# Crossbar DMA transposes in place of TensorE transposes, in a fused sparse-attention and squared-ReLU layer

## The chip, the cores and the metric

The kernel runs on one core of a Trainium2 chip. A core has five instruction streams: TensorE (PE, matrix products into PSUM), VectorE (DVE), ScalarE (ACT), GpSimd (POOL) and SyncE (SP), and sixteen DMA engines [...]. The metric is the device time of one execution in microseconds (us); lower is better.

## The reference

Two steps. First, attention over 4 batches, 8 heads, 768 positions and head size 64: a query attends to the 8 first (global) keys and to the 96 keys up to its own position, with a bias that falls linearly with distance. Then a two-layer network on the 3072 x 512 result.

```python
def _attn_ref(q, k, v, n_global, n_local):
    scores = scale * np.matmul(q, k.transpose(0, 1, 3, 2))
    rel = pos[:, None] - pos[None, :]
    is_global = pos[None, :] < int(n_global)          # 8
    is_local = (rel >= 0) & (rel < int(n_local))      # 96
    keep = is_global | is_local
    scores = scores + bias                            # -slope[h] * distance
    scores = np.where(keep, scores, -1000000000.0)
    a = softmax(scores)
    return np.matmul(a, v)

def _moe_ref(x, w_in, w_out):                         # 512 -> 2048 -> 512
    h = np.maximum(x @ w_in, 0.0)
    return h * h @ w_out
```

## The kernel before

The work is cut into eight half batches of 384 positions (three tiles of 128); the code calls one of them `x`, and `x.hb` is its number, 0 to 7. This text calls them h0 to h7. Heads are taken in four pairs (`a` from 0 to 3), since two heads of 64 fill 128 partitions.

For each half batch these steps follow:

- **Loads** (`list_loads`, line 279). Three tiles each of q, k and v are fetched from DRAM by DMAs issued on POOL, which turn fp32 into fp16. q and k go to staging tiles `sq` and `sk` (two buffers), v goes straight to its place. Each tile has position on the partitions.
- **Turning q and k** (`turn`, line 362). Scores need head size on the partitions. TensorE turns six 128 x 128 blocks per pair into a PSUM tile `trp`, and ACT or DVE copies it to `qk` (line 189 is the ACT copy, line 191 the copy on DVE or POOL). Then `fix_k` makes `kb`, on DVE: for each key tile a version in which the first 32 columns are those of tile 0, so that the global keys ride along with the local ones. `fix_v` does the same for v into `vb`, on POOL for h2 and later.
- **Scores and weights** (`score`, line 409). TensorE multiplies k and q blocks into `sp`, ACT takes the exponential (`ex`, line 424), and DVE multiplies by a precomputed mask (`phat`, lines 436 and 440).
- **Attending** (`attend`, line 464). TensorE multiplies by v, which carries a column of ones for the sum; DVE divides (`rec` and `tm`, lines 471 and 473).
- **Turning the output** (`to_x`, line 488). TensorE turns the three blocks of `tm` into a PSUM tile `trx`; ACT or DVE copies it to `xt`, which has features on the partitions.
- **Layer 1** (`layer1`, line 508): sixteen pieces of four matmuls each into `hps`, each piece needing all four pairs of `xt`; ReLU on ACT or DVE (lines 532 and 534), square on DVE (line 543).
- **Layer 2** (`layer2`, line 556): twelve pieces of four matmuls into `yps`; a copy to `y` and a store from SP (line 571).

h0 is worked tile by tile by functions of its own, and the order of everything for h0 and h1 up to 51.8 us is written out by hand (`OPENING`). After that a loop over half batches puts the layers of h*n* (`main`) beside the attention of h*n+1* (`side`); `merge` deals the attention's steps out between the pieces of the layers, and the loads for h*n+1* are listed ahead of it.

What order each engine gets is set by `Plan`. Every step is an `Op` with a price in us for each engine that may do it, a list of steps it needs, and a rank. TensorE's steps keep the order in which they were listed, and so do the loads; for the rest `run` repeatedly takes the step that can start first by those prices, with the lower rank first on a tie, and emits it on the cheapest engine. The prices are numbers in the code. On the chip every engine then runs its instructions in the emitted order, and waits for what each needs. `Ring` objects stand for PSUM buffers: six banks of `big`, two of `att`.

The loads of h*n* wait for the turning of h*n-2*, whose staging tiles they overwrite. In the line `before = [prev.turned[-1]] if prev else []` that is the last TensorE step of `turn`. A new batch's `qk`, `kb`, `v` and `vb` (two buffers) wait for the batch before last.

Of the kernel before, what the change touches and what calls it, by code (L numbers as in the profile page):

```python
# [8 lines left out]
FP32 = mybir.dt.float32  # L9
FP16 = mybir.dt.float16  # L10
# [3 lines left out]
P = 128  # L14
# [125 lines left out]
def kernel(  # L140
# [46 lines left out]
    def copy(e, out, in_):  # L187
        if e == "ACT":
            nc.scalar.copy(out=out, in_=in_)  # L189
        else:  # L190
            eng(e).tensor_copy(out=out, in_=in_)  # L191
# [75 lines left out]
    def list_loads(x):  # L267
        r0 = x.half * HALF
        prev = halves[x.hb - 2] if x.hb >= 2 else None
        before = [prev.turned[-1]] if prev else []  # L270
        vbefore = [halves[x.hb - x.half - 3].attended[-1]] if x.hb >= 4 else []

        def rows(src, name, t):
            def emit(e):
                if getattr(x, name, None) is None and name != "v":
                    setattr(x, name, stage_p.tile([P, HT, H, D], FP16, name=name, tag=name))
                dst = (x.bt.v[:, x.half * HT + t, :, 0:D] if name == "v"
                       else getattr(x, name)[:, t, :, :])
                nc.gpsimd.dma_start(out=dst, in_=src[x.b, :, r0 + t * P:r0 + (t + 1) * P, :]  # L279
                                    .rearrange("h p d -> p h d"))  # L280
            return plan.load(0.62, emit, vbefore if name == "v" else before)

        if x.half == 0:
            def start(e):
                new_batch(x.bt)
                nc.vector.memset(x.bt.v[:, :, :, D:D + 1], 1.0)
            x.bt.op = plan.add({"DVE": 0.1}, start, vbefore, rank=0)
        if x.hb:
            x.q_in = [rows(q, "sq", t) for t in range(HT)]
            x.k_in = [rows(k, "sk", t) for t in range(HT)]  # L290
            x.v_in = [rows(v, "v", t) for t in range(HT)]
        else:
            raw = {n: stage_p.tile([P, HT, H, D], FP32, name=n, tag=n, bufs=1)
                   for n in ("rq", "rk")}
            x.q_in, x.k_in, x.v_in = [], [], []

            def fetch(name, src, t, eng, e, lag):
                op = plan.add({e: 0.5}, lambda e: eng.dma_start(
                    out=raw[name][:, t], in_=src[0, :, t * P:(t + 1) * P, :].rearrange(
                        "h p d -> p h d")), rank=-1)  # L300
                op.lag = lag
                return op

            def cast(dst, name, t, f):
                def emit(e):
                    if getattr(x, dst, None) is None:
                        setattr(x, dst, stage_p.tile([P, HT, H, D], FP16, name=dst, tag=dst))
                    copy(e, getattr(x, dst)[:, t], raw[name][:, t])
                return plan.add({"DVE": 0.42, "ACT": 0.54}, emit, [f], rank=0)
            k0 = fetch("rk", k, 0, nc.scalar, "ACT", 3.5)  # L310
            q0 = fetch("rq", q, 0, nc.sync, "SP", 3.5)
            x.q_in.append(cast("sq", "rq", 0, q0))
            x.k_in.append(cast("sk", "rk", 0, k0))
            for t in range(HT):
                if t:
                    x.q_in.append(rows(q, "sq", t))
                    x.k_in.append(cast("sk", "rk", t, fetch("rk", k, t, nc.sync, "SP", 4.0 + t)))
                if t < 2:
                    x.v_in.append(rows(v, "v", t))
            x.v_in.append(rows(v, "v", 2))  # L320
        for l in x.v_in:
            l.needs.append(x.bt.op)
# [15 lines left out]
    def tiles_before(x):  # L338
        return (1, HT - 1) if x.half == 0 else (HT - 1, NT - 1)

    def fix_v(x):
# [9 lines left out]
        costs = {"POOL": 0.6 + 2.1 * n} if x.hb > 1 else {"DVE": 0.2 + 0.65 * n}  # L351
        x.vb_op = plan.add(costs, emit, x.v_in)

    def turn(x, a):
        state = {}

        def emit(e):
            state["ps"] = trp = ps_att.tile([P, 2, HT, P], FP16, name="trp", tag="att")
            warm(trp.rearrange("p i t c -> p (i t c)"))
            for i, st in enumerate((x.sq, x.sk)):  # L360
                for t in range(HT):
                    nc.tensor.transpose(out=trp[:, i, t, :], in_=st[:, t, 2 * a:2 * a + 2, :],  # L362
                                        identity=ident)
        job = plan.pe(6 * 0.056, emit, x.q_in + x.k_in + [ident_op], [att])

        def evac(i):
            def emit(e):
                copy(e, x.bt.qk[:, i, a, x.half * HALF:(x.half + 1) * HALF],
                     state["ps"][:, i].rearrange("p t c -> p (t c)"))
            return plan.after(job, {"ACT": 0.39, "DVE": 0.31}, emit)  # L370
        ops = [evac(0), evac(1)]
        t0, t1 = tiles_before(x)

        def fix_k(e):
            kt = x.bt.qk[:, 1, a, :].rearrange("p (t c) -> p t c", c=P)
            copy(e, x.bt.kb[:, a, t0 - 1:t1 - 1, GR:P], kt[:, t0:t1, GR:P])
            copy(e, x.bt.kb[:, a, t0 - 1:t1 - 1, 0:GR],
                 kt[:, 0:1, 0:GR].to_broadcast([P, t1 - t0, GR]))
        n = t1 - t0
        costs = {"DVE": 0.2 + 0.08 * n}  # L380
        if x.hb == 0:
            costs["POOL"] = 0.5 + 0.17 * n
        x.turned.append(job)
        x.qk_ops[a] = ops + [plan.add(costs, fix_k, [ops[1]])]

    GROUPS = {
        0: ([(0, 0), (1, 0), (1, 1)], [(2, 0), (2, 1)]),
# [91 lines left out]
    def to_x(x, a):  # L479
        st, norm = x.tm[a]  # L480

        def emit(e):
# [8 lines left out]
        x.x_ops[a] = plan.after(job, {"ACT": 0.39, "DVE": 0.31}, lambda e: copy(  # L491
            e, x.xt[:, a, :], st["trx"].rearrange("p t c -> p (t c)")))


    def layer1(x, ms, c0=0, c1=HALF, k0=0, k1=NCT):
        n = c1 - c0
# [52 lines left out]
    def layer2(x, j, m0):  # L549
        st = x.l2.setdefault(j, {})  # L550

        def emit(e):
            if m0 == 0:
                st["ps"] = ps_big.tile([P, 512], FP32, name="yps", tag="big")
            for m in range(m0, m0 + 4):
                nc.tensor.matmul(st["ps"], lhsT=x.h2[:, m, j * P:(j + 1) * P],  # L556
                                 rhs=w_out_sb[:, m, :], start=m == 0, stop=m == NFT - 1)
        job = plan.pe(4 * 0.216, emit, 
                      [x.h2_ops[max(c for c in x.h2_ops if c <= j * P)][m]
                       for m in range(m0, m0 + 4)] + [w_out_op[m0 // 4]], [big] if m0 == 0 else [])  # L560
        if m0 == 0:
            st["users"] = job.users
        else:
            job.users = st["users"]
            job.users[0].append(job)
        if m0 + 4 == NFT:
            def evac(e):
                y = y_p.tile([P, d_model], FP32, name="y", tag="y")
                copy(e, y, st["ps"])
                r0 = x.hb * HALF + j * P  # L570
                nc.sync.dma_start(out=out[r0:r0 + P, :], in_=y)
            plan.after(job, {"ACT": 0.52, "DVE": 0.63}, evac)

    for x in halves:
        x.turned, x.attended = [], []
# [97 lines left out]
    def tile_to_x(x, t, a0):  # L673
# [13 lines left out]
        for a in (a0, a0 + 1):  # L687
            x.x_ops[a, t] = op

    def attention(x):  # L690
        jobs = [lambda: fix_v(x)]
        for a in range(NPAIR + 3):
            if a < NPAIR:
                jobs.append(lambda a=a: turn(x, a))
            if 0 <= a - 1 < NPAIR:
                jobs.append(lambda a=a - 1: score(x, a))
            if 0 <= a - 2 < NPAIR:
                jobs.append(lambda a=a - 2: attend(x, a))
            if 0 <= a - 3 < NPAIR:
                jobs.append(lambda a=a - 3: to_x(x, a))  # L700
        return jobs

    def merge(main, side, start, stop):
        done = 0
        for i, f in enumerate(main):
            if i >= start:
                want = len(side) if i >= stop else (i - start) * len(side) // (stop - start)
                while done < want:
                    side[done]()
                    done += 1  # L710
            f()
        for f in side[done:]:
            f()

    def l1(x, m0=0):
        return [lambda m=m: layer1(x, [m]) for m in range(m0, NFT)]

    def l2(x):
        return [lambda j=j, m0=m0: layer2(x, j, m0) for j in range(HT) for m0 in range(0, NFT, 4)]
# [38 lines left out]
    for hb in range(1, NHB):  # L758
        x = halves[hb]
        if hb + 1 < NHB:  # L760
            list_loads(halves[hb + 1])
        main = l2(x0)[6:] + l2(x) if hb == 1 else l1(x) + l2(x)
        side = attention(halves[hb + 1]) if hb + 1 < NHB else []
        merge(main, side, 1, len(main) - 3)
    with tc.manual_schedule():
        order = plan.run()

# [34 lines left out]
```

The softmax here doesn't subtract the row's maximum and nothing guards it: scores larger than these inputs give would overflow.

## Time and profile before

| | |
|---|---|
| median of 3 runs | 235.64 us (235.53 to 235.78) |
| profiled execution | 235.26 us, span 233.5 us |
| granted TensorE clock, mean | 0.991 |
| TensorE busy | 221.1 us, 2023 matmuls |
| DVE / ACT / POOL busy | 126.0 / 139.1 / 86.2 us |
| DMA moved | 20.77 MB |

The span is the time from the first to the last instruction of the profiled execution; the execution's own time is 1.8 us more. Busy time is the time in which an engine had an instruction at work. TensorE's instructions are pipelined, so its busy time says that something was in the pipe, not that it ran at its peak. In the rows of groups and timelines, a name like `qk<-trp` is the tile that is written and the one that is read, `L362` the line of the code, and `x3` the number of instructions.

### The profile page before, as it was taken

Reading aid. Unit: us, or ns where it says so; the run is one execution under the profiler, and the core shown is the slowest. Engines: PE = TensorE matmul, PEld = TensorE weight load, DVE = VectorE, ACT = ScalarE, POOL = GpSimd, SP = SyncE. Lnnn points to the kernel's source line nnn. Section 1 sums busy time; section 2 is a strip of 40 time slices with the busy share of each in tenths; the row PEclk is TensorE's granted clock in tenths of the full one; section 3 lists DMA queues with packets and bytes.
Section 4 is the critical chain, followed back from the end, with each engine's and each line's share of the span. In section 5 each row is a group of like instructions: output and inputs, shape, how many; then the busy total and the mean of one; then the engine's idle time right before and its main releaser. Section 6 shows DMA issues by size and latency. Waiting matters only on the chain.

```text
span 233.5 us, 5024 instructions
## 1 busy us (share of the span) xinstructions
PE 221.1 (95%) x2023; PEld 133.8 (57%) x2023; DVE 126.0 (54%) x340; ACT 139.1 (60%) x319; POOL 86.2 (37%) x100
## 2 busy tenths in 40 slices
PE   7675999999999999999999999999999999999993
PEld 6553689654555566556655565556655565556541
DVE  5395799441376279425864279325863279323300
ACT  4693797671564598328961598328961598327521
POOL 8948723894457307670292107560000000000000
PEclk9999799999999999999999999999999999999999
DMA  8999999999159907951099107941002100111012
GB/s 149 168 194 155 200 206 193 156 149 108 45 77 164 148 0 50 162 87 46 0 120 171 49 3 51 162 82 45 3 1 93 45 4 0 48 45 45 0 48 90
DMA packets 82583, 20.77 MB, mean 89 GB/s; under 512 B 75392, under 2 KB 79488, under 8 KB 82560
## 3 DMA queue, kind: packets, MB, share of 16 engines
q0 software_dynamic: 74944, 13.11, 74.5%
q1 hardware_dynamic: 6576, 7.08, 9.1%
q10 hardware_dynamic: 1040, 0.26, 0.5%
q8 instruction: 16, 0.26, 0.5%
q14 instruction: 7, 0.06, 0.1%
HBM read 27.26 MB, written 6.29 MB: 144 GB/s over the span
## 4 chain that ended last, share of the span: by engine, by line
PE 88%; POOL 5%; DMA 4%; DVE 0%; issue 0%; ACT 0%; POOLq 0%
PE hps L508 37%; PE yps L556 36%; PE sp L409 5%; PE trp L362 4%; DMA sk<-in_k_dram 4%; PE av L464 4%; PE trx L488 2%; POOL sq L279 2%; POOL v L279 1%; POOL sk L279 1%; POOL w_in_sb L327 1%; ACT y L189 0%; DVE ident L226 0%; DVE qk L191 0%; POOL dist L220 0%
## 5 line engine op out<-in xcount | busy, mean ns | idle before, releaser
L508 PE MATMUL hps<-xt,w_in_sb 128*128 128x384 f16 (+2 forms) x576 | 93.8, 311 | 0.2 <-DMA w_in_sb<-in_moe_w_in_dram 0.2
L556 PE MATMUL yps<-w_out_sb,h 128*128 128x512 f16 x384 | 91.9, 379 | 0.0
L508 PEld LDWEIGHTS <-w_in_sb 128*128 128x128 f16 x576 | 51.4, 99 | 27.7 <-DMA w_in_sb<-in_moe_w_in_dram 0.4
L532 ACT ACTIVATE hr<-hps 128x384 f16<-128x384 f32 (+1 forms) x109 | 56.3, 517 | 12.0 <-PE hps L508 9.8
L543 DVE TENSOR_TENSOR h<-hr 128x768 f16<-128x768 f16 (+1 forms) x68 | 36.8, 541 | 38.0 <-ACT hr L532 36.9
L556 PEld LDWEIGHTS <-h 128*128 128x128 f16 x384 | 34.5, 98 | 33.6
L424 ACT ACTIVATE ex<-sp 128x384 f16<-128x384 f32 x112 | 44.4, 510 | 4.2 <-PE sp L409 4.1
L189 ACT COPY y<-yps 128x512 f32<-128x512 f32 x22 | 12.9, 585 | 55.1 <-PE yps L556 55.1
L279 POOL DMA_DIRECT2D sq<-in_q_dram x23 | 20.8, 914 | 38.0 <-PE trp L362 36.5
L189 ACT COPY qk<-trp 128x384 f16<-128x384 f16 (+1 forms) x43 | 19.9, 506 | 11.4 <-DVE qk L191 10.4
L191 POOL COPY vb<-v 32x520 f16<-32x520 f16 (+3 forms) x18 | 19.3, 1070 | 19.1 <-DMA v<-in_v_dram 18.5
L279 POOL DMA_DIRECT2D v<-in_v_dram x24 | 21.4, 918 | 7.3 <-DMA w_out_sb<-in_moe_w_out_dram 3.3
L279 POOL DMA_DIRECT2D sk<-in_k_dram x21 | 18.6, 908 | 5.9 <-DMA w_out_sb<-in_moe_w_out_dram 3.1
L440 DVE TENSOR_TENSOR phat<-ex,mask 128x768 f16<-128x768 f16 x32 | 16.4, 553 | 5.4 <-ACT ex L424 5.1
L191 DVE COPY qk<-trp 128x384 f16<-128x384 f16 (+1 forms) x19 | 6.9, 365 | 17.5 <-PE trp L362 13.4
L473 DVE TENSOR_TENSOR tm<-av,rec 128x384 f16<-128x384 f32 x28 | 15.6, 557 | 1.0
L464 PEld LDWEIGHTS <-phat 128*128 128x128 f16 x312 | 13.2, 98 | 4.8
L464 PE MATMUL av<-v,phat 128*128 128x65 f16 x192 | 13.2, 193 | 0.0
L436 DVE TENSOR_TENSOR phat<-ex,mask 128x768 f16<-128x768 f16 (+1 forms) x24 | 10.7, 486 | 3.6 <-ACT ex L424 3.5
L464 PE MATMUL av<-vb,phat 128*128 128x65 f16 x120 | 12.1, 193 | 0.0
L191 DVE COPY kb<-qk 128x96 f16<-128x96 f16 (+4 forms) x58 | 10.2, 222 | 3.5 <-ACT qk L189 2.0
L362 PE MATMUL trp<-ident,sk 128*128 128x128 f16 x84 | 10.0, 226 | 1.5 <-DMA sk<-in_k_dram 1.5
(59 smaller groups left out, 154.8 us busy)
## 6 DMA issues: line engine op xcount, KB each, us to landing
out_dram<-y SPq DMA_DIRECT2D x24, 256.0 KB, 2.0
v<-in_v_dram POOLq DMA_DIRECT2D x24, 128.0 KB, 6.3
sq<-in_q_dram POOLq DMA_DIRECT2D x23, 128.0 KB, 5.8
sk<-in_k_dram POOLq DMA_DIRECT2D x21, 128.0 KB, 5.9
w_in_sb<-in_moe_w_in_dram POOLq DMA_DIRECT2D x4, 512.0 KB, 9.0
w_out_sb<-in_moe_w_out_dram POOLq DMA_DIRECT2D x4, 512.0 KB, 14.3
rk<-in_k_dram SPq DMA_DIRECT2D x2, 256.0 KB, 6.2
rk<-in_k_dram ACTq DMA_DIRECT2D x1, 256.0 KB, 4.6
```

Source lines behind the costliest of these rows:

```text
L189: nc.scalar.copy(out=out, in_=in_)
L191: eng(e).tensor_copy(out=out, in_=in_)
L279: nc.gpsimd.dma_start(out=dst, in_=src[x.b, :, r0 + t * P:r0 + (t + 1) * P, :] .rearrange("h p d -> p h d"))
L362: nc.tensor.transpose(out=trp[:, i, t, :], in_=st[:, t, 2 * a:2 * a + 2, :], identity=ident)
L424: nc.scalar.activation(out=st["ex", g][:, h, 0:n], in_=st[g][h][:, 0:n], func=AF.Exp, scale=scale)
L440: eng(e).tensor_tensor(out=phat[:, :, c0:c0 + n].rearrange("p e (i c) -> p e i c", c=P), in0=ex[:, :, 0:n].rearrange("p e (i c) -> p e i c ...
L464: nc.tensor.matmul(av[:, h, j, :], lhsT=phat[:, h, c * P:(c + 1) * P], rhs=rhs, start=n == 0, stop=n == len(mine) - 1)
L473: nc.vector.tensor_tensor(out=st["tm"].rearrange("p t e d -> p e t d"), in0=av[:, :, :, 0:D], in1=rec[:, :, :, None].to_broadcast([P, 2, H ...
L508: nc.tensor.matmul(st["ps"][:, i * n:(i + 1) * n], lhsT=w_in_sb[:, kk, m * P:(m + 1) * P], rhs=x.xt[:, kk, c0:c1], start=kk == 0, stop=kk ...
L532: nc.scalar.activation(out=o, in_=i, func=AF.Relu)
L543: eng(e).tensor_tensor(out=x.h2[:, m0:m0 + width, c0:c1], in0=hr, in1=hr, op=ALU.mult)
L556: nc.tensor.matmul(st["ps"], lhsT=x.h2[:, m, j * P:(j + 1) * P], rhs=w_out_sb[:, m, :], start=m == 0, stop=m == NFT - 1)
```

## The change

q and k of h2 to h7 are no longer turned by TensorE. `turn_by_dma` issues six DMAs for each half from SP, one for each tile of q and of k, each of which turns a 128 x 512 block from staging straight into `qk` (all four pairs at once) [...]. The outputs of h3 to h7 are turned in the same way by `to_x_by_dma`, four DMAs of 128 x 384 for each half. The PSUM tiles `trp` and `trx` and their copies fall away for these halves. h1's turning, and the outputs of h0 to h2, stay on TensorE.

With that, `fix_k` becomes a function of its own, which may only run on DVE, and needs all six DMAs of its half. The turning and `fix_v` of h*n+1* are listed right after its loads, ahead of `merge`. The loads wait for all turning DMAs of h*n-2*. `merge` now places the attention's steps at fractions of `main`: the scores of pair `a` at 0.02 + 0.16 a, attending 0.17 later, turning the output 0.3 after the scores, so that the last is listed at 0.80. The store of `y` becomes a step of its own on SP, since SP's order now matters.

```diff
     def list_loads(x):
...
-        before = [prev.turned[-1]] if prev else []
+        before = prev.turned if prev else []
...
+    def fix_k(x, a):
+        t0, t1 = tiles_before(x)
+
+        def emit(e):
+            kt = x.bt.qk[:, 1, a, :].rearrange("p (t c) -> p t c", c=P)
+            copy(e, x.bt.kb[:, a, t0 - 1:t1 - 1, GR:P], kt[:, t0:t1, GR:P])
+            copy(e, x.bt.kb[:, a, t0 - 1:t1 - 1, 0:GR],
+                 kt[:, 0:1, 0:GR].to_broadcast([P, t1 - t0, GR]))
+        return {"DVE": 0.2 + 0.08 * (t1 - t0)}, emit
...
+    def turn_by_dma(x):
+        r0 = x.half * HALF
+        ops = []
+        for t in range(HT):
+            for i, (src, loads) in enumerate((("sq", x.q_in), ("sk", x.k_in))):
+                def emit(e, i=i, t=t, name=src):
+                    nc.sync.dma_start_transpose(
+                        out=x.bt.qk[:, i, :, r0 + t * P:r0 + (t + 1) * P],
+                        in_=getattr(x, name)[:, t].rearrange("p h d -> p (h d)"))
+                op = plan.add({"SP": 1.2}, emit, [loads[t], x.bt.op])
+                op.lag = 2.5
+                ops.append(op)
+        x.turned += ops
+        for a in range(NPAIR):
+            x.qk_ops[a] = ops + [plan.add(*fix_k(x, a), ops)]
...
+    def to_x_by_dma(x, a):
+        st, norm = x.tm[a]
+
+        def emit(e):
+            if x.xt is None:
+                x.xt = h_p.tile([P, NCT, HALF], FP16, name="xt", tag="xt")
+            nc.sync.dma_start_transpose(
+                out=x.xt[:, a, :].rearrange("p (t c) -> p t c", c=P),
+                in_=st["tm"].rearrange("p t e d -> p (t e d)"))
+        x.x_ops[a] = plan.add({"SP": 1.2}, emit, [norm])
+        x.x_ops[a].lag = 2.5
...
             def evac(e):
-                y = y_p.tile([P, d_model], FP32, name="y", tag="y")
-                copy(e, y, st["ps"])
-                r0 = x.hb * HALF + j * P
-                nc.sync.dma_start(out=out[r0:r0 + P, :], in_=y)
-            plan.after(job, {"ACT": 0.52, "DVE": 0.63}, evac)
+                st["y"] = y_p.tile([P, d_model], FP32, name="y", tag="y")
+                copy(e, st["y"], st["ps"])
+            r0 = x.hb * HALF + j * P
+            y_op = plan.after(job, {"ACT": 0.52, "DVE": 0.63}, evac)
+            plan.add({"SP": 0.6}, lambda e: nc.sync.dma_start(out=out[r0:r0 + P, :], in_=st["y"]),
+                     [y_op])
...
     def attention(x):
-        jobs = [lambda: fix_v(x)]
-        for a in range(NPAIR + 3):
-            if a < NPAIR:
-                jobs.append(lambda a=a: turn(x, a))
-            if 0 <= a - 1 < NPAIR:
-                jobs.append(lambda a=a - 1: score(x, a))
-            if 0 <= a - 2 < NPAIR:
-                jobs.append(lambda a=a - 2: attend(x, a))
-            if 0 <= a - 3 < NPAIR:
-                jobs.append(lambda a=a - 3: to_x(x, a))
-        return jobs
+        jobs = []
+        for a in range(NPAIR):
+            jobs.append((0.02 + 0.16 * a, lambda a=a: score(x, a)))
+            jobs.append((0.02 + 0.16 * a + 0.17, lambda a=a: attend(x, a)))
+            turn_x = to_x_by_dma if x.hb > 2 else to_x
+            jobs.append((0.02 + 0.16 * a + 0.3, lambda a=a, turn_x=turn_x: turn_x(x, a)))
+        return sorted(jobs, key=lambda j: j[0])
 
-    def merge(main, side, start, stop):
-        done = 0
+    def merge(main, side):
         for i, f in enumerate(main):
-            if i >= start:
-                want = len(side) if i >= stop else (i - start) * len(side) // (stop - start)
-                while done < want:
-                    side[done]()
-                    done += 1
+            while side and side[0][0] * len(main) <= i:
+                side.pop(0)[1]()
             f()
-        for f in side[done:]:
-            f()
+        for _, g in side:
+            g()
...
         if hb + 1 < NHB:
             list_loads(halves[hb + 1])
+            fix_v(halves[hb + 1])
+            turn_by_dma(halves[hb + 1])
         main = l2(x0)[6:] + l2(x) if hb == 1 else l1(x) + l2(x)
         side = attention(halves[hb + 1]) if hb + 1 < NHB else []
-        merge(main, side, 1, len(main) - 3)
+        merge(main, side)
```

More of the change, by code (lines that the diff above doesn't have):

```diff
@@ L371, in turn @@
         ops = [evac(0), evac(1)]
[L372 to L382, printed above, removed]
-        x.turned.append(job)
-        x.qk_ops[a] = ops + [plan.add(costs, fix_k, [ops[1]])]
+        x.turned.append(job)
+        x.qk_ops[a] = ops + [plan.add(*fix_k(x, a), [ops[1]])]
+    def turn_by_dma(x):
[13 more added lines that the diff above has]
+            x.qk_ops[a] = ops + [plan.add(*fix_k(x, a), ops)]
     GROUPS = {
```

## The prediction

> **What bounds the kernel now.** I read the busy shares first, then the picture of the span in 40 slices. TensorE (PE) is busy for 95 per cent; from the sixth slice (about 29 us) on it is full, while the others swing.
>
> ```profile
> PE 221.1 (95%) x2023; PEld 133.8 (57%) x2023; DVE 126.0 (54%) x340; ACT 139.1 (60%) x319; POOL 86.2 (37%) x100
> PE   7675999999999999999999999999999999999993
> DMA  8999999999159907951099107941002100111012
> ```
>
> A busy engine can hide gaps, so I asked for the chain that ended last in one period alone, 130 to 156 us: the two layers of one half batch and, beside them, the attention of the next. Its sums hold only TensorE, no wait and no DMA. What leaves TensorE here leaves the time, unless a new wait takes its place.
>
> ```profile
> by line: PE hps L508 41.2%; PE yps L556 39.4%; PE sp L409 6.8%; PE av L464 5.6%; PE trp L362 5.2%; PE trx L488 2.6%
> ```
>
> The timeline of TensorE from 130 us gives the price of a transpose. Each row shows start and length; lengths overlap because matmuls are pipelined, so the starts are what counts: from 132.57 to 132.91 us six transposes, 57 ns each.
>
> ```profile
> 132.57 0.33 PE L362 MATMUL trp<-ident,sq 128*128 128x128 f16 x3
> 132.74 0.33 PE L362 MATMUL trp<-ident,sk 128*128 128x128 f16 x3
> 132.91 1.46 PE L508 MATMUL hps<-xt,w_in_sb 128*128 128x384 f16 x8
> ```
>
> The page's list of DMA issues and the timeline of POOL show what the new DMAs will stand beside. A load takes about 0.9 us of POOL and lands 6 us after its issue; a store, alone on its queue, lands in 2.0 us. The copy of v (line 191) stands on POOL between loads and waits for a landing: the 2.89 us in brackets.
>
> ```profile
> out_dram<-y SPq DMA_DIRECT2D x24, 256.0 KB, 2.0
> v<-in_v_dram POOLq DMA_DIRECT2D x24, 128.0 KB, 6.3
> ...
> sk<-in_k_dram POOLq DMA_DIRECT2D x21, 128.0 KB, 5.9
> ```
>
> ```profile
> 56.74 4.52 POOL L191 COPY vb<-v 32x1560 f16<-32x1560 f16 x3 [2.89 <-DMA v<-in_v_dram]
> 66.68 2.63 POOL L279 DMA_DIRECT2D sq<-in_q_dram  x3 [5.42 <-PE trp L362]
> 69.27 2.66 POOL L279 DMA_DIRECT2D sk<-in_k_dram  x3
> ```
>
> [...] k loads issued from 30 to 60 us, in the crowd, landed in 8.6 us (median), those from 86 to 100 us in 4.6.
>
> **The change, part by part.** Half batches are called h0 to h7.
>
> *TensorE.* Gone are the transposes of q and k for h2 to h7 (24 each) and those of the outputs for h3 to h7 (12 each): 144 + 60 = 204, which is also the number of matmuls missing in the built order. By shares of the 26 us period: 5.2% is 1.35 us a half, times 6 is 8.1; 2.6% is 0.68, times 5 is 3.4. Sum **-11.5 us**, on the path. The 204 times 56 ns of the timeline give 11.4; I take 11.4.
>
> *ACT and DVE.* The PSUM copies of these transposes go (8 a half for q and k, 4 for outputs; ACT 478 ns, DVE 357 ns each). In the period ACT is busy 16.6 and DVE 15.6 of 26 us, all behind TensorE: worth nothing. The two copies into kb per pair stay on DVE; they now wait for a DMA instead of a copy.
>
> *SP.* Before, it held only 24 stores and early fetches. Now 36 transposes of 128 KB (q, k) and 20 of 96 KB (outputs) join, in one queue in order. Each waits for its load (or its normalisation) and the stores queue behind. The store's separate plan entry only puts it in this order. Price of a transpose: unknown. [...] I take the planner's own price in the diff, 1.2 us of SP and 2.5 us more to landing, which is no measurement. The total on SP is then about 36 x 1.2 + 20 x 1.0 = 63 us over some 150 us: it fits.
>
> *Outputs.* In the built order the last attention of a half is followed by 36 layer-2 matmuls, 36 x 0.216 = 7.8 us, before the next half's first layer needs all four transposes. Normalising takes 0.2 + 0.56 us plus hops, about 1.0; a transpose 3.7; 3 us are over. Hidden, and it stays hidden up to some 6.5 us of latency; beyond that each us costs five halves 1 us each. Earlier pairs are 3.3 us apart, so SP has time for them.
>
> *q and k: the turn is early, the loads are late.* h2 is safe: its loads are issued by 37 us, its first score now comes at 51.83 + 28 x 0.216 = 57.9 us. But the order of DVE is fixed by the planner, and it puts the kb copies of h4 and h5 well ahead of their use, in front of work that TensorE needs at once. What is queued behind them: normalising h2's last pair, then squares, weights and normalising for h3. h4: POOL reaches most of its loads after the v copy that ends at 56.74 + 4.52 = 61.3 us; five loads at 0.9 end at 65.8; the last k lands 5.4 us after its issue, 70.3; 3.7 more is 74.0. The four kb copies take 1.1 (0.27 a pair), the normalising 0.8, so the output transpose of h2's last pair (still on TensorE) can start at 75.9. TensorE would be there at 73.3 (57.9 plus 56 layer-2 matmuls at 0.216, four scores at 0.39, four attentions at 0.31 and three output turns at 0.17): **+2.6 us**. h5: POOL issues v of h4 and q of h5 until 71.1, waits for v (67.6 + 6.1 = 73.7), copies 2.2, issues k until 78.5; that lands at 83.0, and is turned at 86.7. Layer 1 of h2 starts at 73.3 + 0.2 + 2.6 + 2.6 = 78.7 (12 more layer-2 matmuls, the first stall), and the copies stand some 5 us into it, behind the second square: DVE is there at about 83.5. From the copies to the weights of h3's second pair it has 3.2 us of work, to 89.9, against 87.2 on TensorE (8.5 us into layer 1): **+2.7 us**. For h6 and h7 SP itself is held back by h3's outputs, and their copies stand as far behind; TensorE is then 12 us later than the plan thought and I cost them at nothing. [...] with landings 2 us later they come to 7 or 8.
>
> *Attention in the first 80 per cent.* The same TensorE work in another place: nothing, as ACT and DVE have a third of each period free. That cover is what the outputs' 7.8 us pay for.
>
> Sum, against the profiled execution (235.26 us; span 233.5 and 1.8 around): 235.26 - 11.4 + 5.3 = 229.2. That execution stands 0.4 below the median shown, so **229.5 us**.
>
> **Rivals.**
> *Nothing waits.* The loads land as the planner supposes, or DVE's waits fall where TensorE has slack: 235.6 - 11.4 = 224.2. For it: in the trace DVE often waits 4 us for ACT at no cost. Against: the v copies on POOL delay k, as worked out.
>
> *Slower: SP's queue becomes the bound.* The mechanism is the price T of a 128 KB transpose[...]. From about 43 us (k of h2 landed) to DVE's copies for h7 (about 122 us), 36 T + 8 x 0.75 T + 9 x 0.6 for stores must fit into 79 us: T up to 1.75 us. Each 0.1 us above is 4.2 us more; from T = 1.9 the change loses, at 2.5 us it gives about 229 + 31 = 260[...]. For it: nothing in this trace shows the operation[...]. [...]
>
> *The outputs arrive late.* A latency of 8 us instead of 3.7 costs 5 x 1.5: 237; to land above 235.3 it needs over 7.7. Small, as it takes slow landing with a fast queue.
>
> That the change does not do what it says is out: in the built order the 204 matmuls are gone and 56 transposes stand on SP.
>
> **How the numbers follow.** About 0.2% (0.5 us) is what a measurement here can tell from no change. Chances: forecast with some stall (225.5 to 234.8) 0.42; nothing waits (223.5 to 225.5) 0.22; stall as large as the gain, within 0.2%, 0.03; SP's queue 0.28, of which half below 250; late outputs 0.05. So faster 0.64, same 0.03, slower 0.33. The range from 223.5 to 250 leaves out the slow half of the queue case and a little: 2 in 10. The faster cases alone span 223.5 to 234.8.
>
> **What would show it.** Right: TensorE's count lower by 204, no trp in periods after h1; DMA rows for SP's transposes with about 1.2 us between issues and some 3 us to landing; DVE waits on qk between 71 and 90 us, and TensorE's two gaps there, then periods of about 24 us with no gap. Wrong: gaps on TensorE before the first layer of each half (late outputs), SP's transposes back to back through the middle with DVE waiting on them (queue), or no gap at 71 to 90 us (nothing waits).

## The result, and the profile after

The changed kernel takes **243.75 us** (median of 4 runs, 242.28 to 245.45) against 235.71 us for the kernel before (4 runs beside it, 235.53 to 236.65): a ratio of 1.0335, 95% interval 1.0263 to 1.0408. It is slower by 8.0 us; 229.5 was forecast. Its profiled execution took 243.63 us, with a span of 241.8.

The page after, busy shares and slices:

```profile
PE 215.7 (89%) x1819; PEld 123.9 (51%) x1819; DVE 119.5 (49%) x311; ACT 123.9 (51%) x280; POOL 86.1 (36%) x100
PE   7664999999169679699999999999999999999993
PEclk9999799999859958799999999999999999999999
DMA  8999999999999999972999933102111211021012
```

The 204 matmuls are gone. But the slice that starts at 60 us holds a 1 where there was a 9, others up to 100 us are not full, and the row PEclk (granted TensorE clock in tenths) drops behind each hole. From about 100 us on all slices are full. The DMA engines, which before were nearly idle in slices around 60 and 85 us, are now full without a break up to about 100 us. The chain by line from 160 to 217 us shows that the saving is real: there is no `trp` and no `trx` in it.

```profile
by line: PE yps L584 51.1%; PE hps L536 37.2%; PE av L480 6.1%; PE sp L425 5.8%
```

In that chain, first layers start at 144.85, 168.93, 192.88 and 217.29 us: periods of 24.0 to 24.4 us, where the kernel before took 26. So the loss is all ahead of about 102 us. TensorE's timeline there (start, length, form, count; in brackets the idle time before and what ended it):

```profile
68.74 0.57 PE L480 MATMUL av<-v,phat 128*128 128x65 f16 x4 [7.37 <-DVE phat L452]
...
69.46 2.93 PE L584 MATMUL yps<-w_out_sb,h 128*128 128x512 f16 x8
...
74.05 1.89 PE L584 MATMUL yps<-w_out_sb,h 128*128 128x512 f16 x8
...
79.75 0.34 PE L504 MATMUL trx<-ident,tm 128*128 128x128 f16 x3 [0.26 <-DVE tm L489]
...
86.31 0.50 PE L504 MATMUL trx<-ident,tm 128*128 128x128 f16 x3 [3.32 <-DVE tm L489]
86.60 5.33 PE L584 MATMUL yps<-w_out_sb,h 128*128 128x512 f16 x12
...
97.43 0.20 PE L480 MATMUL av<-v,phat 128*128 128x65 f16 x1 [0.49 <-DVE phat L456]
99.18 0.23 PE L480 MATMUL av<-vb,phat 128*128 128x65 f16 x1 [1.55 <-DVE phat L456]
```

**The account.** The gaps sum to 7.37 + 0.26 + 3.32 + 0.49 + 1.55 = 13.0 us. Behind them the same work runs slower: eight `yps` matmuls took 2.93 us at 69.46 and 1.89 at 74.05, twelve took 5.33 at 86.60 and 2.75 at 109.33, sixteen `hps` 3.99 at 99.78 and 2.76 at 104.52. That is 1.0 + 2.6 + 1.2 = 4.8, and smaller groups beside them bring it to about 6 (by the windows of the trace the clock was at half for 2.8, 5.7 and 3.1 us of work, and half of their sum is 5.8). So -11.4 + 13.0 + 6 = +7.6, of the 8.4 between the two profiled executions; 0.8 stays unassigned.

**What made the gaps.** The chain that ended last, in order of time (start, length, engine or DMA):

```profile
45.91 12.80 DMA sk<-in_k_dram
58.73 1.19 SPq L392
...
61.32 4.69 DMA qk<-sk
...
66.13 2.41 DVE kb L191 x6
68.53 0.16 DVE phat L452
68.74 0.91 PE av L480 x10
...
76.86 7.67 DMA qk<-sk
84.55 1.08 DVE kb L191 x8
85.69 0.57 DVE tm L489
```

A k load of h3 takes 12.8 us to land, SP turns what came late, and the `kb` copies of h3 stand on DVE in front of the `phat` that TensorE needs for h2. In the kernel before, the three k loads of h3, issued from 46.1 to 47.8 us, landed in half that time:

```profile
DMA to landing us min/median/max: 6.8/6.9/6.9
```

The same happens with h4 at 84.55, in front of h2's last `tm`. Here are those copies in DVE's timeline, and a third place where something else happened:

```profile
66.13 2.41 DVE L191 COPY kb<-qk 128x288 f16<-128x288 f16 x6 [8.90 <-DMA qk<-sk]
...
84.55 1.08 DVE L191 COPY kb<-qk 128x96 f16<-128x96 f16 x8 [4.87 <-DMA qk<-sk]
...
95.54 3.59 DVE L456 TENSOR_TENSOR phat<-ex,mask 128x768 f16<-128x768 f16 x2
```

DVE did nothing for 8.90 and 4.87 us. The six copies at 66.13 took 2.41 us beside POOL's `vb` copies (63.09 to 67.67 us); in e10 below, which moves those, the same six took 0.85, so some 1.6 of the 7.4 us are of that kind. The third place is taken up below. The list of DMA issues gives times from issue to landing (last column, median); the two `qk` rows are from the full list of DMAs.

```profile
sq<-in_q_dram POOLq DMA_DIRECT2D x23, 128.0 KB, 10.8
sk<-in_k_dram POOLq DMA_DIRECT2D x21, 128.0 KB, 8.1
...
xt<-tm SPq DMA_TRANSPOSE x20, 2.3
```

```profile
qk<-sq SPq DMA_TRANSPOSE x18, 7.1
qk<-sk SPq DMA_TRANSPOSE x18, 7.7
```

SP's issue is 1.19 us in the chain above and 1.28 in the median of all 36 (six took 1.7 to 3.0), about as taken. But q and k transposes land 7 us after the start of their issue, not the 3.7 (1.2 and 2.5) of the prediction, while those of the outputs, most of which come after the loads have ended, land after 2.3. The loads are slower too: q 10.8 us where the same row said 5.8 before.

### The profile page after: what moved, and what is told of

It is laid out like the page before. It is cut to its first block, busy times and chain, and to the rows that moved or that the text cites. A ratio compares the mean times of both kernels' runs of the same rounds, so it can differ in the third digit from the quotient of the medians.

```text
span 241.8 us, 4686 instructions
## 1 busy us (share of the span) xinstructions
PE 215.7 (89%) x1819; PEld 123.9 (51%) x1819; DVE 119.5 (49%) x311; ACT 123.9 (51%) x280; POOL 86.1 (36%) x100
## 3 DMA queue, kind: packets, MB, share of 16 engines
q1 hardware_dynamic: 34480, 13.77, 29.5%
## 4 chain that ended last, share of the span: by engine, by line
PE 62%; DMA 20%; DVE 6%; POOL 5%; SPq 4%; ACT 2%; issue 1%; DVEq 0%; POOLq 0%
PE hps L536 28%; PE yps L584 25%; DMA sk<-in_k_dram 10%; DMA qk<-sk 9%; PE av L480 4%; PE sp L425 4%; SPq L392 3%; DVE kb L191 3%; POOL sq L279 2%; DVE phat L456 1%; POOL v L279 1%; DMA xt<-tm 1%; ACT ex L440 1%; PE trp L372 1%; POOL sk L279 1%
## 5 line engine op out<-in xcount | busy, mean ns | idle before, releaser
L536 PE MATMUL hps<-xt,w_in_sb 128*128 128x384 f16 (+2 forms) x576 | 92.3, 313 | 0.9 <-DMA w_in_sb<-in_moe_w_in_dram 0.7
L584 PE MATMUL yps<-w_out_sb,h 128*128 128x512 f16 x384 | 89.9, 391 | 0.0
L536 PEld LDWEIGHTS <-w_in_sb 128*128 128x128 f16 x576 | 52.2, 99 | 30.6 <-issue 2.1
L584 PEld LDWEIGHTS <-h 128*128 128x128 f16 x384 | 37.5, 100 | 43.9 <-issue 4.1
L189 ACT COPY y<-yps 128x512 f32<-128x512 f32 x23 | 13.5, 587 | 77.4 <-PE yps L584 77.4
L562 DVE TENSOR_SCALAR hr<-hps 128x384 f16<-128x384 f32 x14 | 7.8, 555 | 37.1 <-PE hps L536 36.6
L191 DVE COPY kb<-qk 128x96 f16<-128x96 f16 (+4 forms) x58 | 14.4, 334 | 21.4 <-DMA qk<-sk 20.7
L480 PE MATMUL av<-v,phat 128*128 128x65 f16 x192 | 14.1, 198 | 7.9 <-DVE phat L452 7.4
L456 DVE TENSOR_TENSOR phat<-ex,mask 128x768 f16<-128x768 f16 x32 | 19.0, 631 | 0.3 <-ACT ex L440 0.2
L425 PE MATMUL sp<-qk 64*128 64x128 f16 x192 | 10.3, 219 | 0.0
L425 PEld LDWEIGHTS <-qk 64*128 64x128 f16 x192 | 5.5, 94 | 8.4 <-issue 8.0
## 6 DMA issues: line engine op xcount, KB each, us to landing
sq<-in_q_dram POOLq DMA_DIRECT2D x23, 128.0 KB, 10.8
```

Source lines behind the costliest of these rows:

```text
L425: nc.tensor.matmul(pair[h][:, i * P:(i + 1) * P], lhsT=lhsT, rhs=bt.qk[rows, 0, a, r * P:(r + 1) * P], start=True, stop=True)
L456: eng(e).tensor_tensor(out=phat[:, :, c0:c0 + n].rearrange("p e (i c) -> p e i c", c=P), in0=ex[:, :, 0:n].rearrange("p e (i c) -> p e i c ...
L480: nc.tensor.matmul(av[:, h, j, :], lhsT=phat[:, h, c * P:(c + 1) * P], rhs=rhs, start=n == 0, stop=n == len(mine) - 1)
L536: nc.tensor.matmul(st["ps"][:, i * n:(i + 1) * n], lhsT=w_in_sb[:, kk, m * P:(m + 1) * P], rhs=x.xt[:, kk, c0:c1], start=kk == 0, stop=kk ...
```

## The experiments

Theory after the result: `kb` copies stand too early on DVE and wait for turning DMAs; DMA crowding makes these late; the slow clock adds to the gaps. Rivals: the crowding alone is the loss wherever the copies stand; SP's queue; POOL's late `vb` copies, which the prediction had blamed for h4 and h5. Edits are relative to the changed kernel unless told otherwise.

**e1_kb_late: the copies later.** They may only be placed after the last attention of the half before.

```diff
-            x.qk_ops[a] = ops + [plan.add(*fix_k(x, a), ops)]
+            x.qk_ops[a] = ops + [plan.add(*fix_k(x, a), ops + [halves[x.hb - 1].attended[-1]])]
```

> The changed kernel, but each half's copies into kb stand on DVE behind the last attention of the half before, so that nothing which TensorE needs earlier is queued behind them. Order theory: the loss came from DVE standing at these copies while the turning DMAs landed late; TensorE's gaps at 61 to 69, 83 to 86 and 97 to 99 us (13 us in all) and the slower clock after them go, and the time is about 225 to 228 us. Contention theory: loads and turning DMAs share the DMA engines, so q and k themselves are late; the gaps move to the first scores of h3 to h5 and the time stays above 236 us.

Measured: 235.5 us, ratio to the kernel before 0.9981 (0.9959 to 1.0003). Eight of the missing microseconds are back. That is fewer than the order theory said (225 to 228), and the contention theory's 236 or more did not come either. The 7.4 us gap is gone, and two new waits stand in the list of waits of this run (what waited, for what, us, times, longest):

```profile
PE hps L536 <- DMA xt<-tm: 3.6, 3, 2.3
PE hps L536 <- ACT y L189: 2.6, 1, 2.6
```

Both lead to SP, as e5 below bears out: a turning DMA at its head waits for a load, and stores and output transposes stand behind it. A late store holds a `y` buffer, and so ACT's copy; a late `xt` holds layer 1. Removing the block on DVE laid bare one on SP.

**e9_turn_only: the turning later, the copies left.** The issue of a half's turning DMAs waits for the last attention of the half two before.

```diff
-                op = plan.add({"SP": 1.2}, emit, [loads[t], x.bt.op])
+                op = plan.add({"SP": 1.2}, emit, [loads[t], x.bt.op, halves[x.hb - 2].attended[-1]])
```

> The changed kernel with only the second edit of e5: q and k of a half are turned behind the last attention two halves earlier; the copies into kb stand where the planner's prices put them, as in the changed kernel. Order theory: both edits are needed. The first gap (h3's copies, 7.4 us, and the slow clock after it) stays, since h3's turning is not moved; the later copies still stand where a landing after 2.5 us was expected and 7 came. About 234 to 241 us. If SP's order alone were the cause, it would be near e5, 227 to 229.

Measured: 237.59 us, ratio 1.0047 (1.0025 to 1.0069). A gap of 7.23 us at 69.13 stays, of the second only 1.08 is left. Alone, e1 wins back 8.2 us and this edit 6.2; neither is enough.

**e5_turn_late: both edits, e1's and e9's.**

> As e1 (late copies into kb), and besides, the planner puts the turning of q and k of a half behind the last attention two halves earlier, so that SP does not stand at a load that has not landed while stores and output turns are queued behind it. Queue theory: what is left in e1 (235.5 us) are waits behind SP's queue - layer 1 of h2 for a store, 2.6 us at 79 us, and the outputs of h4, 3.3 us and more before 140 us - and the slow clock after them; they go, and the time is 225 to 228 us. Contention theory (the DMA engines themselves are too busy): the waits come back elsewhere and the time stays above 232 us.

Measured: **227.08 us**, ratio 0.9616 (0.9587 to 0.9644); it beats both kernels. From its page:

```profile
PE 210.0 (93%) x1819; PEld 122.2 (54%) x1819; DVE 124.1 (55%) x314; ACT 122.8 (55%) x277; POOL 87.5 (39%) x100
PE   7675799999997999999999999999999999999993
PEclk9999699999999999999999999999999999999999
DMA  7999999999999999999999996154112100220012
```

The large holes are gone (one gap of 1.57 us is left, at 72 us), and the clock stays up, though the DMA engines are full until about 135 us. Between 60 and 150 us the turning DMAs still take 6.5 us to land (median; 7.1 in the changed kernel): they are nearly as late as before, but little that TensorE needs stands behind them. Here the lateness was not the loss by itself; what was queued behind it was.

**e3_qk_only and e2_outs_only: the halves of the change.** The first turns all outputs on TensorE (`to_x`). The second leaves q and k on TensorE:

```diff
-            jobs.append((0.02 + 0.16 * a, lambda a=a: score(x, a)))
+            jobs.append((max(0.0, 0.16 * a - 0.09), lambda a=a: turn(x, a)))
+            jobs.append((0.02 + 0.16 * a if a else 0.08, lambda a=a: score(x, a)))
...
-            turn_by_dma(halves[hb + 1])
```

> Only q and k of h2 to h7 are turned by DMA; all outputs are turned by TensorE. Order theory: the gaps are those of the changed kernel, and 3.4 us more of TensorE work: about 247 us. If the outputs' DMAs, mixed into SP's queue, delay the turning of q and k, the gaps shrink and the time is below 243 us.

> Only the outputs of h3 to h7 are turned by DMA; q and k are turned by TensorE as before, spread ahead of their scores. Order theory: the outputs' part is harmless, with 2.3 us from issue to landing (measured in the changed kernel once the loads are over); 5 x 0.68 = 3.4 us leave TensorE, so about 232 to 233 us and no gap before the first layer of a half. If the outputs' DMAs cost something of their own, it is above 234 us, with gaps there.

Measured: 257.23 us, ratio 1.0929 (1.0852 to 1.1007), and 235.12 us, ratio 0.9963 (0.995 to 0.9976). The loss is all with q and k. With the outputs on TensorE it grows, to ten us more than expected, since the output turns of later halves now stand behind the waiting copies too; the waits of e3:

```profile
DVE kb L191 <- DMA qk<-sk: 24.4, 4, 9.0
...
PE trx L504 <- DVE tm L489: 13.6, 4, 8.0
```

With the outputs alone, the periods that hold the attention of h4 and h6 take 25.3 us (105.96 to 131.25, 157.55 to 182.83) instead of 25.95: there the 0.7 us is won, and hidden as forecast. Those of h3, h5 and h7 are only 0.1 to 0.4 us shorter, with short waits of TensorE for `phat`, so that the five periods together win 2.0 us of the 3.4 expected. And layer 1 of h2 starts 2.1 us later than in the kernel before, 0.9 of it already lost by 42 us, where this edit means to change nothing; that eats the gain. I put the turns just ahead of the scores; whether this place costs the rest is not shown. So this run shows that the outputs do no harm, and not what they can win in the total.

**e4_lag_real: telling the planner.** `op.lag` of the turning DMAs from 2.5 to 8.0.

> The changed kernel, but the planner is told that a turning DMA of q or k lands 8.0 us after SP has issued it (measured: 7.3 us in the median while loads run) instead of 2.5. Order theory with the price as the failing term: the copies move back by 5.5 us on DVE, most of the first gap (7.4 us) goes, less of those of h4 and h5, whose loads are late as well: about 228 to 236 us. If the price is not what matters: within 2 us of the changed kernel, 242 to 246.

Measured: 237.55 us, ratio 1.0077 (1.0056 to 1.0099): 6 us better than the changed kernel. The first gap is down to 0.2 us, and the longest that is left is 2.9, at 103 us. DVE still waits 13.4 us in all for `qk`, 7.9 at longest, probably since the loads' own lateness stays untold. A truer price helps, a dependence (e5) helps more.

**e6_stores_act: stores off SP.** e1, with the stores issued from ACT.

```diff
-            plan.add({"SP": 0.6}, lambda e: nc.sync.dma_start(out=out[r0:r0 + P, :], in_=st["y"]),
+            plan.add({"ACT": 0.6}, lambda e: nc.scalar.dma_start(out=out[r0:r0 + P, :], in_=st["y"]),
```

> As e1, with the stores of y issued from ACT instead of SP. Queue theory: the wait of layer 1 of h2 for ACT's y (2.6 us, with the slow clock after it some 4.5 us) goes, the late outputs of h4 stay, and the stores' issues cost ACT 0.5 us each, hidden: about 230 to 232 us. If the stores are late because the DMA engines are full, nothing changes: 235.

Measured: 248.2 us, ratio 1.0516 (1.048 to 1.0551). Missed. The scores now wait for ACT, as TensorE's timeline shows:

```profile
67.55 1.19 PE L425 MATMUL sp<-qk 64*128 64x128 f16 x8 [5.63 <-ACT ex L440]
```

A second one, of 5.75 us, follows at 80.44. ACT in turn waits 25.8 us in all, three times, for `qk<-sq` DMAs that its exponentials don't read. In ACT's stream the wait that ends just before the exponentials is one of the store's line (L600, at 66.56 and 79.47 us): ACT stands at a store that waits for what the profile takes to be a turning DMA's semaphore. Why the store waits for it is not isolated. What is shown: the queue can't simply be moved to ACT.

**e7_no_loads67: the same transposes without loads beside them.** The loads of h6 and h7 are left out, and their staging and v are those of h4 and h5, so this kernel computes something else; it was run once.

> The changed kernel without any loads for h6 and h7: their q, k and v are those of h4 and h5 again; everything else, the twelve turning DMAs for them included, is done. Contention theory: a turning DMA lands late because it shares the DMA engines with loads, so those of h6 and h7 now land 2.5 to 3.5 us after their issue (6.6 to 10.2 in the changed kernel between 115 and 130 us). If turning DMAs delay each other, several being in flight, they still take 6 us or more.

Measured: 246.27 us; the time is not the point. From issue to landing, for turning DMAs of q and k, first in this run (115 to 128 us), then in the changed kernel (115 to 130 us):

```profile
DMA to landing us min/median/max: 2.4/2.5/2.6
```

```profile
DMA to landing us min/median/max: 6.6/7.9/10.2
```

The same instructions in the same place take a third of the time when the loads are away, 2.5 us against 7.9 in the median (the next one in this run took 4.1 us). Where on the way the two kinds of DMA hold each other up is not shown.

**e8_forced_gap: what a gap costs.** The kernel before, with layer 1 of h5 made to wait for a chain of POOL copies.

```diff
+            if x.gap and ms[0] == 0:
+                nc.tensor.matmul(st["ps"][:, 0:1], lhsT=gap_t[:, 0:P], rhs=gap_t[:, 0:1],
+                                 start=True, stop=True)
...
+            halves[5].gap = [plan.add({"POOL": 11.0}, gap, [x.l2[1]["op"]])]
```

> The kernel before, with one wait put in: ahead of layer 1 of h5 TensorE waits for a chain of copies on POOL, some 11 us long, begun when the second tile of h4's layer 2 has been copied out. Nothing else is changed. Clock theory: [...] the time grows by the gap (about 7 to 8 us) and 2 to 3 us more. If a gap costs only its length, the time grows by the gap as the trace shows it, within 0.5 us.

Measured: 250.14 us, ratio 1.0617 (1.0575 to 1.066). TensorE's timeline, and stretches of 2 us (columns: PE, PEld, DVE, ACT and POOL busy with counts, granted clock, DMA share, GB/s):

```profile
168.33 0.19 PE L508 MATMUL hps<-gap_t 128*128 128x1 f16 x1 [12.40 <-POOL gap_t L776]
168.38 4.19 PE L512 MATMUL hps<-xt,w_in_sb 128*128 128x384 f16 x16
```

```profile
160.00:162.00 2.00, 0.00 (x0) 0.00 (x0) 0.00 (x0) 0.00 (x0) 1.94 (x2) 0.77 0.00 0
...
168.00:170.00 2.00, 1.67 (x7) 0.82 (x8) 0.00 (x0) 0.14 (x1) 0.28 (x1) 0.50 0.00 0
...
172.00:174.00 2.00, 2.00 (x18) 1.34 (x17) 1.19 (x5) 1.60 (x4) 0.00 (x0) 1.00 0.00 0
```

With the DMA share at 0.00 from 160 us on, the clock falls to half some 5 us into the gap (0.77 in the stretch from 160 us, 0.50 in the next) and comes back some 3 us after work resumes (0.67 from 170 us, 1.00 from 172). Sixteen `hps` took 4.19 us here and 2.76 in the kernel before: 1.4 us on top of the gap, where 2 to 3 were expected. (The spans of the two profiled executions, 247.0 and 233.5, differ by 13.5 us for a gap of 12.4.) So here idling alone brought a slow stretch; and in e5 full DMA engines alone brought none: from 50 to 220 us its clock is 1.00 in every stretch of 10 us. The slow stretches of the changed kernel, each behind a gap, are put down to idling on these grounds.

**e10_vb_late: POOL's copies later.** The `vb` copies wait for the last attention of the half before, so that POOL reaches the k loads sooner.

```diff
-        x.vb_op = plan.add(costs, emit, x.v_in)
+        x.vb_op = plan.add(costs, emit, x.v_in + [halves[x.hb - 1].attended[-1]] if x.hb > 1 else x.v_in)
```

> The changed kernel, but POOL's copies of v into vb stand behind the last attention of the half before, so that POOL does not hold up the loads of h4 and h5 for them (and does not copy while DVE weights h3's scores). POOL theory, as in the prediction: the loads of h4 and h5 come some 5 us earlier, the gaps at 83 and 97 us shrink or go, the first gap (h3, 7.4 us) stays: 234 to 239 us. If the loads' order does not matter, because the DMA engines are full anyway, the time stays at 242 to 246 us.

Measured: 248.28 us, ratio 1.051 (1.0472 to 1.0548), with gaps of 8.05, 3.19 and 3.18 us. Missed: the k loads of h4 were issued 8 to 9 us sooner (from 60.2 us instead of 69.4) and landed only 3 to 5 us sooner, and beside them the turned k of h3 landed 2.7 us later, so that the longest wait of `kb` grew from 8.9 to 11.3 us. Taking POOL's copies out of the loads' way does not bring the turning in time.

**e11_best and e12_y5: can e5 be bettered?** e12 is e5 with five `y` buffers instead of three, against its only gap left, 1.57 us behind a late store. e11 also turns the outputs of h2 by DMA.

> As e5, with five buffers for y instead of three, so that no copy out of PSUM waits for a store held up on SP, and the outputs of h2 turned by DMA too. Queue theory: the one wait left in e5 (1.6 us at 72 us, a store behind h3's turning) goes, and 0.7 us of TensorE work: 224 to 226 us. If h2's outputs on SP get stuck behind the turning of h3 and h4, TensorE waits ahead of layer 1 of h2 and the time is 227 us or more.

> As e5, with five buffers for y instead of three; the outputs of h2 stay on TensorE. Queue theory: the wait of 1.6 us that was left in e5 at 72 us came through DVE's copy of y, held for a store behind h3's turning on SP; it goes, and the time is 225 to 226.5 us. If e11 was slow through the buffers and not through h2's outputs landing late, it is above 230 us.

Measured: e12 227.49 us, ratio 0.9632 (0.9603 to 0.966); e11 235.64, ratio 0.9988 (0.9968 to 1.0008). In e12 that wait falls to 0.26 us, but the opening, which the edit does not mean to touch, ends 1 us later, and the intervals of e5 and e12 overlap: no gain is shown. In e11 h2's outputs land in the loads' crowd, and TensorE's timeline shows layer 1 waiting for them:

```profile
83.64 0.48 PE L536 MATMUL hps<-xt,w_in_sb 128*128 128x384 f16 x1 [3.78 <-DMA xt<-tm]
```

So leaving h2's outputs on TensorE is right here: they were not hidden in the loads' crowd (h0 and h1 were not tried). e5 stays the best version.

## Why the prediction was wrong, step by step

**Right.** *The saving*: 204 transposes, 11.4 us; periods of 24.0 to 24.4, and e5 comes within 3 us of 235.7 - 11.4 = 224.3. *SP's issue* of 1.2 us (1.28 in the median), so the slower rival, SP's price T above 1.9 us, did not come. (Its bound on T starts at 43 us with h2's k landed; in the trace before that k landed at 44.6 to 46.4. Nothing hangs on it.) *The outputs hidden*: only 0.2 us of waits for `xt` in the changed kernel. *The mechanism of the loss*: `kb` copies placed early on DVE, normalising and weights of h2 behind them. The stall for h4 stands where it was put in the order, with 3.3 us for a forecast 2.6; that closeness is luck, since both sides of it came ten us late: the turned k at 84.5 us and not 74.0, TensorE at 83.0 and not 73.3.

**The step that failed first: the landings, priced as if loads and turns did not hold each other up.** I took 3.7 us from the start of the issue to landing for a turn. Beside the loads it was 7.3 (median of the 36), and where the loads are over or left out even less than I took: 2.3 for outputs and 2.5 in e7. I also took the loads' 5.4 and 6.1 us over from a kernel without the transposes; with them, 8 to 11. Side by side both landed later, and I priced each as if the other stayed as it was. I had the loads' 8.6 us in the crowd and 4.6 outside it from the trace before, and let that difference enter no sum.

**The second, which follows from it: "h2 is safe", with h3 never costed.** I counted from h4 on. h3's copies stood in front of h2's weights, and that gap, 7.4 us, is the largest single term. But costing h3 by my prices would not have found it: in the trace before, h3's last k landed at 54.7 us, so by an estimate from that trace it would be turned at 58.4 and copied by 59.5, while TensorE ran out of other work only at 61.4. In the changed kernel that k landed at 61.0, and the turned block that the copies waited for at 66.0. The term that was mis-sized is the landing, not only the half that was left out.

**The third: no term for the clock.** In e8 the clock fell to half some 5 us into the gap of 12.4, and came back some 3 us after its end. The changed kernel is harsher: the 3.3 us gap was followed by 0.50 up to 92 us, and two gaps of 0.49 and 1.55 us at 97 to 99 by 0.72 and 0.50 up to 102, so idling of 2 us in two pieces was enough here (the single gap of 1.57 us in e5 was not: 1.00 from 70 to 80 us). It cost about 6 us, half of the gaps' own length.

**The fourth: POOL as the cause of late k for h4 and h5.** e10 refutes it as a remedy: h4's stall stayed, with 3.19 us. h5's 2.7 us did not come in that form: its copies at 99.52 did not wait. The 2.0 us lost just before belong to two `phat` of 1.83 us each (usually 0.55), while POOL's `vb` copies ran from 93.72 to 98.71 us: a wait that no rival of the prediction had.

The direction turned on these sizes: 5.3 us of stalls were forecast, against a saving of 11.4, and 13.0 of gaps and 6 of slow clock came. The slower rival had the sign right for a wrong reason: what cost the time was the queues' order (DVE's, then SP's) behind late landings, not the price on SP.

## What to carry to other kernels

A DMA that replaces engine work can cost more than it saves when an instruction placed in front of other work waits for it: 243.75 us in the changed kernel, where the turns landed after 7.1 us (60 to 150 us), against 227.08 in e5, where they still took 6.5. Go through the first consumer of every moved transfer, the first instances above all, and ask what stands behind it on its engine, and behind the issue on the queue. Price a small DMA by its landing among the transfers that will run beside it (here 7.9 us and not 2.5), and those by it (q loads 10.8 and not 5.8). Add to the gaps on TensorE the work at half clock behind them: in the changed kernel some 6 us for 13.0 us of gaps, in e8 1.4 for 12.4.

## What the runs showed of the hardware that was not expected

- A DMA transpose from SBUF takes SP some 1.2 us (medians 1.28 for q and k, 1.18 for outputs). With no loads beside it, it landed 2.3 us (128 x 384 fp16, median of the outputs, most of them behind the last load) or 2.4 to 2.6 us (128 x 512, e7) after the start of its issue; beside converting loads 6.6 to 10.2 us (115 to 130 us in the changed kernel). SP's queue moved 34,480 packets where the kernel before had 6,576. By the packet sizes in the two traces, the 27,904 more are 26,112 of 256 bytes, which is 512 for each 128 KB and 384 for each 96 KB, and 1,792 of 4 bytes, 32 for each of the 56 DMAs.
- A gap of 12.4 us on TensorE (e8) cost 1.4 us more than itself. In the changed kernel the gap of 7.4 us was followed by 2.8 us of work at half clock, that of 3.3 by 5.7, and 2.0 in two pieces by 3.1: the shorter gap did not cost less.
- A DVE product of two SBUF tiles (128 x 768) took 1.83 us instead of 0.55 beside POOL's `vb` copies. In the changed kernel no other of its 56 `phat` took over 0.56, and it is so in other runs (e9: one `h` of 1.83 us). e10, which moves POOL's copies, has the `phat` of h3 at 0.55, and two at 128.69 us, beside POOL's copies (126.11 to 131.18 us), at 2.76 together. That ties the slow ones to POOL's copies; by what they hold DVE up is not shown.
